# Attention into a gated unit: exponentials of one local piece by ScalarE group by group, and the first block's list of work made anew

## The chip, the cores and the metric

The kernel runs on one core of a Trainium2 chip, as one program with one launch. Its time is the device time in microseconds (us) of an execution; the median of several executions is what counts. Engines are named as in the profile: PE is TensorE with its matmuls (PEld its weight loads), DVE is VectorE, ACT is ScalarE, POOL is GpSimd, SP is SyncE, which issues the loads.

## The reference

Eight batches of eight heads of attention over 576 positions with 64 columns a head, four heads with a band of 32 positions and four that see every 32nd position; the result of all heads side by side, 4608 rows of 512, goes through a gated unit with 1536 hidden columns. All of it is float32.

```python
scores = scale * np.matmul(q, k.transpose(0, 1, 3, 2))
mask_local = (rel >= 0) & (rel < stride)
mask_strided = (rel >= 0) & (pos[None, :] % stride == pos[:, None] % stride)
scores = np.where(masks[None, :, :, :], scores, -1000000000.0)
scores = scores - np.max(scores, axis=-1, keepdims=True)
attn = np.exp(scores)
attn = attn / (np.sum(attn, axis=-1, keepdims=True) + 1e-09)
x = np.matmul(attn, v)            # then to (B * S, H * D)
gate = 1.0 / (1.0 + np.exp(-(x @ w_gate)))
return (gate * (x @ w_val)) @ w_out
```

## The kernel before, in words

**Attention by pieces.** A batch has four pieces, b.0 to b.3, each two heads: 0 and 2 are local, 1 and 3 strided. The positions that see each other are laid out so that a local piece has ten groups of 64 columns (five per head) on 128 partitions, a strided piece twelve groups of 54. Each group has a maximum and a sum of its own per partition. A piece goes through steps: Q and V load queries with keys, and values; K writes the mask into a PSUM bank by a matmul (first batch; for later ones DVE adds it, step M); S multiplies the scores onto it; A takes the maxima (DVE, one instruction for all ten groups); U subtracts them (DVE, into the SBUF tile sb); E takes the exponentials (ACT, one pass over sb, or two if the piece is in parts); N sums the groups and takes reciprocals (DVE); W multiplies (DVE, Wp on POOL); T transposes on PE and P copies out of PSUM (ACT); X weighs the values (PE); H and L split the result into a high and a low part, tiles xh and xl; R keeps the 64 positions beyond 512. In the first batch a local piece has one more column per group that holds 1e-9 (TINY), so that the sum of 65 columns has it in it; step Z sets it by a memset on POOL.

**The products.** A product with float32 weights is three matmuls in a faster type, high by high, low by high and high by low: a triple, 512 columns wide, for each of four chunks of 128 input columns. A weight block is loaded by SP (raw, 512 KB), and split by ACT, DVE and POOL in six steps (wa, wb, ws, wd, wu, wl) into a high and a low tile. Step fg f.i.c is the triple of chunk c for hidden block f, gate (i = 0) or value (i = 1); chunk order is 0, 2, 1, 3, so a product begins when piece 0 is weighed, and needs piece 1 next, then piece 2. Gate and value of a block are followed by the sigmoid and product (s, m), split (x, y) and the product with the third weight (o). Batches 3 to 7 use sums of weights to do with 7 half products what takes 8.

**What sets the order.** All steps stand in one hand-written list of names, ORDER, and each engine runs its instructions in the order in which the steps issue them; nothing else reorders them. SP's queue is the loads in list order. Step J n on PE is a matmul of n columns of ones whose result is not read: it fills time in which PE would have nothing to do. BANKS says which PSUM bank a step of the first batches uses. The first list lines hold the first two batches' attention and the first products and weights; from batch 3 on the list is regular.

The lines that the change and the steps below touch: load_qk L292, load_v L305, room L324, rows L333, soft_max L404, soft_sub L413, expo L431, norm_row L437, norm_sum L444, norm_mult L453, score L360 (matmul L371), turn L463, spread L482, weigh L493, split_high L547, split_low L551, keep_rest L559, products L587 (matmul L592), busy L722 (matmul L730), the splitting of weights L252 to L276, and the table of steps from L947 with the loop that runs the list behind it.

Of the kernel before, what the change touches and what calls it, by code (L numbers as in the profile page):

```python
# [10 lines left out]
F32 = mybir.dt.float32  # L11
# [11 lines left out]
P = 128  # L23
# [41 lines left out]
    "S0.0": "o0", "T0.0": "o1", "X0.0": "o1", "S0.1": "o1", "T0.1": "o0", "X0.1": "o0", "S0.2": "o1", "X0.2": "o1", "T0.3": "o0", "X0.3": "o0",  # L65
    "S1.0": "o1", "X1.0": "o1", "g1": "a",
# [16 lines left out]
wb0.1 wa0.1 fg1.0.0 fH0.2 ws0.1 wr3.0 wb1.1 fT0.3 fL0.2 wa1.1 wd0.1 fR0.2 wr3.2 ws1.1 fg0.0.1 fP0.3 wd1.1 fS1.0 wu0.1 wu1.1 wl0.1 wb0.2 wlp1.1 fg1.0.1
fM1.0 fQ1.1 wa0.2 fg0.1.0 fA1.0 wr4.0 fg0.0.2 wa2.1 fU1.0 fg0.1.1 wb2.1 ws2.1 fX0.3 fE1.0 wr4.2 ws0.2 wdp2.1 wb1.2 fn1.0 fg1.1.0 fH0.3 fN1.0 wu2.1
fg0.1.2 fL0.3 fWp1.0 wa1.2 fg1.1.1 fR0.3 ws1.2 wr5.0 fg1.0.2 wlp2.1 fB1.0.1 fg0.0.3 fg0.1.3 fB1.0.0 s0.0 wdp0.2 fg1.0.3 wb2.2 m0.0 wa2.2 fg1.1.2
wdp1.2 fB1.0.2 x0.0 wr5.1 fg2.0.0 s0.1 fg2.1.0 y0.0 wu0.2 fg2.0.1 wu1.2 fB1.0.3 wa3.0 fg1.1.3 wb3.0 ws2.2 fZ1.1 fg2.1.1 m0.1 wdp2.2 wr5.2 fg2.0.2
# [96 lines left out]
TINY = 1e-9  # L183
# [4 lines left out]
def attention_then_glu(ctx, tc, qk_l, qk_s, v_l, v_s, w_all, consts, out):  # L188
# [89 lines left out]
    def pair(b, step, space):  # L278
# [789 lines left out]
```

## Time and profile before

| | us |
|---|---|
| runs shown (3) | 926.85, 927.66, 929.27 |
| median | 927.66 |
| profiled execution | 929.75 |
| its span | 927.6 |
| PE busy | 919.8 (99% of the span) |
| DVE busy | 599.9 (65%) |
| ACT busy | 426.8 (46%) |
| POOL busy | 179.9 (19%) |
| mean granted clock of PE | 0.996 |

The span runs from the first to the last instruction of the profiled execution; the 2.15 us between it and the execution's time lie around it. In rows of the timeline the first number is the start in us from the span's beginning, the second the time to the group's end, then engine, line, operation, what it writes and reads, and in brackets the idle time before it with what ended it. Rows of groups show in place of the start and time the busy time and the mean ns of one instruction. PE's granted clock is given as a share of full speed.

### The profile page before, as it was taken

To read this page: it belongs to the slowest core of one execution; us is meant where nothing else is said; L and a number is where in the kernel's file an instruction comes from. 1 tells how busy PE (TensorE), PEld (TensorE's weight loads), DVE (VectorE), ACT (ScalarE), POOL (GpSimd) and SP (SyncE) were. 2 spreads that over 40 slices of the span, in tenths; PEclk is the share of its full clock that TensorE was granted. 3 is DMA by queue.
4 is the path that set the end of the run, shared out by engine and by line. 5 is a ranking of instruction groups with operands and counts; after the bars stand their busy time and mean duration, and the time that the engine had idled before them with its cause. 6 is when DMAs were issued, how large, how long until landed. Compare 5 with 4: busy or idle time off the path is not lost.

```text
span 927.6 us, 18516 instructions
## 1 busy us (share of the span) xinstructions
PE 919.8 (99%) x7606; PEld 754.9 (81%) x7606; DVE 599.9 (65%) x959; ACT 426.8 (46%) x776; POOL 179.9 (19%) x243
## 2 busy tenths in 40 slices
PE   8999999999999999999999999999999999999998
PEld 5788888888888888888888888888888888888886
DVE  5898877667799899665667896766248333333331
ACT  5888754334546455443435544444335233332222
POOL 4452641554555321000000210000003000000000
PEclk9899999999999999999999999999999999999999
DMA  9862644465677455655645436654443055444111
GB/s 345 333 220 85 197 152 153 159 192 159 199 240 247 115 187 191 208 189 181 193 157 181 149 109 195 198 181 148 138 156 125 23 174 178 145 150 146 59 45 46
DMA packets 90195, 154.19 MB, mean 166 GB/s; under 512 B 5888, under 2 KB 40192, under 8 KB 90112
## 3 DMA queue, kind: packets, MB, share of 16 engines
q1 hardware_dynamic: 89712, 152.36, 50.9%
q8 instruction: 60, 0.98, 0.4%
q10 hardware_dynamic: 400, 0.66, 0.3%
q14 instruction: 23, 0.19, 0.1%
HBM read 121.53 MB, written 31.46 MB: 165 GB/s over the span
## 4 chain that ended last, share of the span: by engine, by line
PE 98%; ACT 1%; DVE 1%; issue 0%; POOL 0%; DVEq 0%; ACTq 0%; POOLq 0%
PE o L623 22%; PE p L887 21%; PE d L887 16%; PE g L592 10%; PE v L592 10%; PE o_a L623 5%; PE o_g L623 3%; PE o_v L623 3%; PE x_a L513 2%; PE x L513 1%; PE s_g L371 1%; PE s_v L371 1%; PE gv L592 1%; PE s L371 1%; PE unread L730 0%; ACT sb L435 0%
## 5 line engine op out<-in xcount | busy, mean ns | idle before, releaser
L887 PE MATMUL p<-xs,ring 128*128 128x512 f32 x864 | 204.6, 389 | 0.0
L887 PEld LDWEIGHTS p<-xs,ring 128*128 128x128 f32 x864 | 162.2, 188 | 33.7
L623 PE MATMUL o<-w,hh 128*128 128x512 f32 x576 | 180.6, 395 | 0.0
L887 PE MATMUL d<-xs,ring 128*128 128x512 f32 x648 | 155.6, 389 | 0.0
L887 PEld LDWEIGHTS d<-xs,ring 128*128 128x128 f32 x648 | 121.6, 188 | 25.2
L623 PEld LDWEIGHTS o<-w,hh 128*128 128x128 f32 x576 | 106.1, 188 | 22.7
L480 DVE STREAM_TRANSPOSE pt<-sb 32x320 f32<-32x320 f32 (+1 forms) x224 | 120.1, 536 | 4.5
L623 PE MATMUL o<-w,hl 128*128 128x512 f32 x288 | 112.0, 389 | 0.0
L921 DVE TENSOR_TENSOR e<-e,d 128x512 f32<-128x512 f32 x54 | 37.1, 687 | 110.6 <-PE d L887 62.5
L592 PE MATMUL g<-xh,w 128*128 128x512 f32 x256 | 85.9, 393 | 0.0
L916 ACT COPY e<-p 128x512 f32<-128x512 f32 x54 | 31.7, 587 | 116.8 <-PE p L887 116.8
L592 PE MATMUL v<-xh,w 128*128 128x512 f32 x256 | 85.2, 390 | 0.0
L623 PEld LDWEIGHTS o<-w,hl 128*128 128x128 f32 x288 | 54.1, 188 | 11.5
L592 PEld LDWEIGHTS g<-xh,w 128*128 128x128 f32 x256 | 48.5, 189 | 10.3
L592 PEld LDWEIGHTS v<-xh,w 128*128 128x128 f32 x256 | 48.0, 188 | 10.0
L815 POOL TENSOR_TENSOR sum<-sum 128x128 f32<-128x128 f32 x96 | 51.5, 540 | 6.3
L592 PE MATMUL g<-xl,w 128*128 128x512 f32 x128 | 50.3, 393 | 0.3 <-DVE xl L553 0.3
L616 DVE TENSOR_TENSOR hl<-hid,hh 128x512 fp32r<-128x512 f32 x36 | 28.0, 780 | 34.5 <-ACT hh L612 34.3
L592 PE MATMUL v<-xl,w 128*128 128x512 f32 x128 | 49.8, 389 | 0.0
L810 POOL TENSOR_TENSOR sum<-w 128x256 f32<-128x256 f32 x44 | 35.5, 827 | 72.7 <-DMA sets<-sum 49.4
L929 ACT ACTIVATE e<-e 128x512 f32<-128x512 f32 x54 | 34.2, 633 | 29.9 <-DVE e L921 29.9
L612 ACT CAST hh<-hid 128x512 fp32r<-128x512 f32 x36 | 22.4, 622 | 49.9 <-PE o_a L623 41.1
(164 smaller groups left out, 1416.6 us busy)
## 6 DMA issues: line engine op xcount, KB each, us to landing
ring<-sets SPq DMA_DIRECT2D x126, 512.0 KB, 4.1
raw<-in_w_all SPq DMA_DIRECT2D x36, 512.0 KB, 5.8
vv<-in_v_l SPq DMA_DIRECT2D x15, 640.0 KB, 4.6
qk<-in_qk_l SPq DMA_DIRECT2D x14, 608.0 KB, 5.2
qk<-in_qk_s SPq DMA_DIRECT2D x14, 594.0 KB, 6.0
out<-ob SPq DMA_DIRECT2D x32, 256.0 KB, 2.0
sets<-w SPq DMA_DIRECT2D x24, 256.0 KB, 3.3
sets<-sumh SPq DMA_DIRECT2D x24, 256.0 KB, 2.8
```

Of the source, the lines that this page charges most:

```text
L371: nc.tensor.matmul(sc[j % len(sc)][g * m : (g + 1) * m, j // len(sc) * BANK + (s - lo) * kk : j // len(sc) * BANK + (s - lo + 1) * kk], q[ ...
L480: nc.vector.transpose(dst[to : to + LB, :, col : col + LB], src[part * LB : (part + 1) * LB, :, h * LB : (h + 1) * LB])
L513: nc.tensor.matmul(at_bank(r, (u * per + g) * m, (u * per + g + 1) * m)[j * D : (j + 1) * D], v[part][rows, slot * P + j * D : slot * P + ...
L592: nc.tensor.matmul(o, w, x, start=first and n == 0, stop=last and n == len(todo) - 1)
L616: by.tensor_tensor(hl, whole_h.pop((k, f)), hh.bitcast(F32), op=ALU.subtract)
L623: nc.tensor.matmul(acc[k][i], h[:, i * P : (i + 1) * P], w, start=f == 0 and n == 0, stop=f == NF - 1 and n == 2,)
L810: nc.gpsimd.tensor_tensor(u[:, at : at + 2], part(wh[f][i], c), part(wl[f][i], c), op=ALU.add)
L815: nc.gpsimd.tensor_tensor(u[:, to], u[:, x], u[:, y], op=op)
L887: nc.tensor.matmul(to, w[:, (wi * 2 + c) * P : (wi * 2 + c + 1) * P], x[xi][:, c], start=p in (1, 2, 5) and c == j == 0, stop=c == 1 and j ...
L916: nc.scalar.copy(x, two[m, 0])
L921: nc.vector.tensor_tensor(x, x, two[m, 1], op=ALU.add)
L929: nc.scalar.activation(x, x, AF.Sigmoid)
```

## The change

In piece 2 of batch 0 (local) DVE no longer subtracts the maxima and no longer sums. A step G (max_neg, POOL) writes minus scale times the maxima into columns of mxs, which is twice as wide; then the step E finds them and does, in place of one pass over sb, ten activations of 64 columns each. Each reads its scores from PSUM, has its column of negated maxima as the bias, writes its group of sb, and adds the group's exponentials up into a column (accum_out). POOL adds TINY to the ten sums. Step N of that piece is then only DVE's reciprocal. The other pieces take the old path. Step Z with its memset is as it was.

```diff
 BANKS = {
-    "S0.0": "o0", "T0.0": "o1", "X0.0": "o1", "S0.1": "o1", "T0.1": "o0", "X0.1": "o0", "S0.2": "o1", "X0.2": "o1", "T0.3": "o0", "X0.3": "o0",
-    "S1.0": "o1", "X1.0": "o1", "g1": "a",
+    "Sa0.0": "o0", "X0.0": "o0", "S0.1": "o1", "T0.1": "o0", "S0.2": "o0", "S0.3": "o0", "T0.3": "o1", "S1.0": "o1", "S1.1": "o1", "g1": "o0",
 }
...
-fAa0.0 wr1.1 fSa0.1 fA0.0 fQ1.0 wr0.2 fUa0.0 wr2.1 fS0.1 fU0.0 fEa0.0 wr1.2 fK0.3 fE0.0 fA0.1 wb2.0 wa2.0 fU0.1 wr4.1 fN0.0 fE0.1 J1024 fK0.2 fS0.2 fN0.1
...
+fP0.1 wa2.0 wd0.1 J384 fK0.2 wu0.0 ws2.0 fS0.2 wu0.1 wlp0.0 wb2.0 fX0.1 fA0.2 wr4.1 fN0.3 fH0.1 fG0.2 wlp0.1 fE0.2 J224 fS1.0 fL0.1 fWp0.3 fg0.1.0 fQ1.1 fM1.0
+fg0.0.0 fA1.0 wdp2.0 fR0.1 fN0.2 wb1.0 fW0.2 wa1.0 wu2.0 ws1.0 wr3.1 fT0.2 wb2.1 wd1.0 wlp2.0 fg0.1.1 fP0.2 fU1.0 wu1.0 fT0.3 fg1.1.0 fP0.3 fX0.2
...
-    mxs = pool.tile([P, 64], F32, name="mxs")
+    mxs = pool.tile([P, 128], F32, name="mxs")
...
+        def max_neg():
+            row = rows()[1]
+            neg = mxs[:, 64 + 16 * step : 64 + 16 * step + 2 * ns]
+            nc.gpsimd.tensor_scalar_mul(neg, row, -SCALE)
+            todo["neg"] = neg
+
+        def expo_groups():
+            prob, row, _ = rows()
+            scores = scores_of(None).rearrange("p j (t k) -> p j t k", k=kk)
+            neg = todo.pop("neg")
+            for j in range(2):
+                for t in range(ns):
+                    n = j * ns + t
+                    nc.scalar.activation(
+                        prob[:, n], scores[:, j, t], AF.Exp, bias=neg[:, n : n + 1], scale=SCALE, accum_out=row[:, n : n + 1]
+                    )
+            nc.gpsimd.tensor_scalar_add(row, row, TINY)
+            todo["row"] = row
+            todo["tiny"] = True
+
...
         def expo(part=None):
+            if "neg" in todo:
+                return expo_groups()
             prob = rows()[0]
...
             row = todo.pop("row")
-            if wide == kk:
+            if wide == kk and "tiny" not in todo:
                 nc.vector.tensor_scalar_add(row, row, TINY)
             nc.vector.reciprocal(row, row)
...
-        fE=in_parts("E"), fn=first_steps("NR"), fN=first_steps("NS"), ...
+        fG=first_steps("G"), fE=in_parts("E"), fn=first_steps("NR"), fN=first_steps("NS"), ...
```

The list is made anew from its first name up to where batch 2's products begin, and in parts behind that; later only a few of the steps e and d (copying a result out and storing it) trade places. The columns of J sum to 3552 before and 3136 now. What the list does to the engines is seen in the rows below, an engine's instructions in program order. A name ends in the piece and a buffer's number (t0_2 is the transposed block of batch 0, piece 2; qk1_0 the queries and keys of batch 1, piece 0; x the weighed values; v0_0, g0_0 and gv0_1 products).

On PE, from the first transposes of piece 2 on, before:

```order
L513 MATMUL x0_0_380<-pt0_0_271,vv0_0_127 64x32 x36
L467 MATMUL t0_2_429<-ident_62,pt0_2_342 128x128 x4
L471 MATMUL t0_2_429<-ident_62,pt0_2_342 64x64 x2
L592 MATMUL g0_0_446<-xh0_75,w0_0_377 128x512
L592 MATMUL g0_0_446<-xl0_76,w0_0_377 128x512
L592 MATMUL g0_0_446<-xh0_75,w0_0_377 128x512
L513 MATMUL x0_2_452<-pt0_2_342,v0_2_132 64x32 x32
L513 MATMUL x0_2_452<-pt0_2_342,u0_2_134 64x32 x4
L592 MATMUL gv0_1_494<-xh0_75,w1_0_340 128x512
L592 MATMUL gv0_1_494<-xl0_76,w1_0_340 128x512
```

And now, from the weighing of piece 1 on:

```order
L534 MATMUL x0_1_393<-pt0_1_340,vv0_1_180 64x54 x22
L751 MATMUL unread_82<-ones_80 128x224
L370 MATMUL s1_0_444<-qk1_0_203 32x64 x40
L613 MATMUL v0_0_489<-xh0_75,w0_1_389 128x512
L613 MATMUL v0_0_489<-xl0_76,w0_1_389 128x512
L613 MATMUL v0_0_489<-xh0_75,w0_1_389 128x512
L613 MATMUL g0_0_498<-xh0_75,w0_0_350 128x512
L613 MATMUL g0_0_498<-xl0_76,w0_0_350 128x512
L613 MATMUL g0_0_498<-xh0_75,w0_0_350 128x512
L488 MATMUL t0_2_519<-ident_62,pt0_2_511 128x128 x4
```

The transposes of piece 2 stood ahead of the first triple; now the scores of the next batch's piece 0 (40 matmuls from qk1_0) and two triples, for value and gate, stand ahead of them. Before, those scores came behind the first three triples.

On DVE, the stretch that holds piece 2's multiplication (pt0_2), before, from the maxima of piece 2:

```order
L409 TENSOR_REDUCE mxs_63<-s0_2_230 128x10
L418 TENSOR_TENSOR sb0_2_96<-s0_2_230,mxs_63 128x10x64
L265 TENSOR_SCALAR high1_0_273<-high1_0_273 128x512
L265 TENSOR_SCALAR words2_0_219<-words2_0_219 128x512
L441 TENSOR_REDUCE mxs_63<-sb0_2_96 128x10
L451 RECIPROCAL mxs_63<-mxs_63 128x10
L265 TENSOR_SCALAR high0_0_320<-high0_0_320 128x512
L409 TENSOR_REDUCE mxs_63<-s0_3_214 128x12
L459 TENSOR_TENSOR pt0_2_342<-sb0_2_96,mxs_63 128x640
```

And now, from the same maxima:

```order
L408 TENSOR_REDUCE mxs_63<-s0_2_347 128x10
L462 TENSOR_REDUCE mxs_63<-sb0_3_93 128x12
L472 RECIPROCAL mxs_63<-mxs_63 128x12
L574 TENSOR_TENSOR xl0_76<-x0_1_393,xh0_75 128x16x18
L574 TENSOR_TENSOR xl0_76<-x0_1_393,xh0_75 128x16x12
L574 TENSOR_TENSOR xl0_76<-x0_1_393,xh0_75 128x16x2
L389 TENSOR_TENSOR sb1_0_495<-s1_0_444,cst_61 128x640
L410 TENSOR_REDUCE mx1_0_496<-sb1_0_495 128x10
L472 RECIPROCAL mxs_63<-mxs_63 128x10
L480 TENSOR_TENSOR pt0_2_511<-sb0_2_96,mxs_63 128x640
```

Subtraction and sum of piece 2 are gone; its reciprocal and multiplication now stand behind the low part of piece 1, and behind the mask and the maxima of the next batch's piece 0 (sb1_0, mx1_0).

On ACT, the ten groups in their place now:

```order
L570 CAST xh0_75<-x0_1_393 128x16x18
L570 CAST xh0_75<-x0_1_393 128x16x12
L570 CAST xh0_75<-x0_1_393 128x16x2
L439 ACTIVATE sb0_2_96,mxs_63<-s0_2_347,mxs_63 128x64 x10
L583 COPY xr0_77<-x0_1_393 128x2x18
L583 COPY xr0_77<-x0_1_393 128x2x12
```

The ten groups, shown as one row, are behind the casts of piece 1 and ahead of its left-over columns; their rows wait for POOL's multiplication by minus scale.

On SP, the loads from the first values on, before:

```order
L316 DMA vv0_1_122<-in_v_s 128x768
L316 DMA vv0_0_127<-in_v_l 128x1280
L312 DMA v0_2_132<-in_v_l 128x1024
L312 DMA u0_2_134<-in_v_l 128x256
L312 DMA v0_3_161<-in_v_s 128x768
L236 DMA raw0_1_163<-in_w_all 128x1024
L236 DMA raw1_1_178<-in_w_all 128x1024
L303 DMA qk1_0_193<-in_qk_l 128x1216
```

And now:

```order
L315 DMA vv0_1_180<-in_v_s 128x768
L311 DMA v0_2_183<-in_v_l 128x1024
L311 DMA u0_2_185<-in_v_l 128x256
L302 DMA qk1_0_203<-in_qk_l 128x1216
L311 DMA v0_3_206<-in_v_s 128x768
L235 DMA raw1_0_209<-in_w_all 128x1024
```

The queries of batch 1 (qk1_0) stood behind five weight blocks and the values of all four pieces; they now stand behind four weight blocks (raw1_1, raw0_1, raw0_0 and raw2_0) and the values of pieces 0 to 2. The values of piece 3 and block raw1_0 come right after them.

More of the change, by code (lines that the diff above doesn't have):

```diff
@@ L83 @@
[L83 to L86, printed above, removed]
@@ L131 @@
[L131 removed]
+J0 K fZ0.0 fZ0.1 fQa0.0 fZ0.3 fZ0.2 fQb0.0 fQa0.1 fQb0.1 fQ0.3 C J384 fK0.1 fK0.0 wr1.1 fKa0.0 fV0.0 fQ0.2 fSa0.0 wr0.1 wr0.0 fS0.0 fAa0.0 wr2.0 fSa0.1 fV0.1
+fUa0.0 fV0.2 fA0.0 fEa0.0 fS0.1 fU0.0 fK0.3 fQ1.0 fA0.1 fV0.3 fE0.0 wr1.0 fN0.0 wr2.1 J352 fS0.3 wr0.2 wr1.2 fWp0.0 fA0.3 wa1.1 fU0.3 wb1.1 J576 fT0.0 fU0.1
+fE0.3 wr3.2 ws1.1 fP0.0 fE0.1 wd1.1 J320 fX0.0 wu1.1 fN0.1 wlp1.1 fH0.0 fV1.0 fR0.0 wb0.1 fL0.0 wa0.1 fW0.1 wa0.0 wr3.0 ws0.1 J896 fT0.1 wb0.0 ws0.0 wd0.0 wr2.2
@@ new lines @@
+y0.9 o0.8 wu11.0 ws10.2 wlp11.0 fL1.2 fB1.3.3 s0.10 wdp10.2 wa11.1 fg10.1 wb11.1 ws11.1 wu10.2 wd11.1 wlp10.2 fB1.3.2 o0.9 m0.10 wu11.1 x0.10 wl11.1
+y0.10 wa11.2 fB1.3.0 wb11.2 fg11.0 fB1.3.1 ws11.2 wd11.2 fg11.1 s0.11 wu11.2 wlp11.2 fX1.3 pa0.0.1 m0.11 o0.10 fH1.3 LV0 x0.11 fL1.3 pb0.0.1 fR1.3
+y0.11 g1.0 pa0.0.0 pb0.0.0 pl0 v1.0 s1.0 oh0.11.0 m1.0 x1.0 S0.0 e0.0 y1.0 d0.0 oh0.11.1 LQ1 M0.0 M0.1 D0 A0 g1.1 e0.2 U0 d0.2 e0.1 E0 d0.1 N0 v1.1
+s1.1 W0 e0.3 g1.2 ph0.0.0.1 d0.3 m1.1 B0.1 x1.1 y1.1 ph0.0.1.0 B0.0 v1.2 s1.2 B0.2 B0.3 o1.0 Z1 m1.2 pw0.0.0 x1.2 pw0.0.1 pd0.0.0 y1.2 pd0.0.1 X0.0
@@ new lines @@
+oh2.2.0 m2.3 Z7 pw4.1.1 x2.3 X6.0 pw5.0.0 pd4.1.1 y2.3 pd5.0.0 S7.0 LV7 H6 R6 xh3.1.1 oh2.2.1 LQ8 M7.0 M7.1 pa5.0.1 A7 g2.4 D7 U7 pa5.1.0 xl3.1.1 E7
+pb5.0.1 N7 v2.4 s2.4 W7 pb5.1.0 ph5.0.1.1 B7.0 g2.5 m2.4 B7.1 x2.4 ph5.1.0.0 B7.2 v2.5 B7.3 y2.4 pw5.0.1 s2.5 oh2.3.0 pw5.1.0 pd5.0.1 m2.5 pd5.1.0
+X7.0 x2.5 y2.5 S8.0 LV8 H7 R7 pa5.1.1 oh2.3.1 xh3.1.2 LQ9 M8.0 M8.1 A8 o2.4 pb5.1.1 D8 U8 xl3.1.2 E8 ph5.1.1.1 N8 g2.6 W8 B8.0 v2.6 s2.6 B8.1 B8.2
+B8.3 oh2.5.0 m2.6 Z9 pw5.1.1 X8.0 x2.6 pd5.1.1 y2.6 S9.0 LV9 H8 R8 xd3.0.0 oh2.5.1 LQ10 M9.0 M9.1 D9 A9 g2.7 xh3.0.5 U9 xl3.0.5 E9 N9 v2.7 s2.7 W9
@@ new lines @@
+xd3.1.2 xl3.1.3 D12 xh3.1.6 A12 xh3.1.7 xl3.1.6 xl3.1.7 o2.11 xd3.1.3 U12 e2.0 xh3.1.4 d2.0 e2.1 E12 xl3.1.4 d2.1 G3.0.1 N12 e2.2 V3.0.1 W12 d2.2
+c3.0.0.1 B12.0 G3.0.2 r5 c3.0.1.1 B12.1 V3.0.2 ad3.0.0.2 B12.2 sg3.0.2 G3.0.6 r6 ad3.0.1.2 mu3.0.2 V3.0.6 c3.0.0.6 B12.3 x3.0 G3.0.5 r7 c3.0.1.6 y3.0
+Z13 e2.3 V3.0.5 d2.3 G3.0.7 r8 V3.0.7 c3.0.0.7 ad3.0.0.7 G3.0.4 c3.0.1.7 sg3.0.7 ad3.0.1.7 V3.0.4 sg3.0.4 mu3.0.7 G3.0.3 r9 mu3.0.4 x3.1 V3.0.3
+ad3.0.0.3 y3.1 sg3.0.3 oh3.0.0 r10 ad3.0.1.3 mu3.0.3 X12.0 S13.0 LV13 H12 R12 oh3.0.1 LQ14 M13.0 M13.1 D13 A13 G3.1.1 U13 V3.1.1 c3.1.0.1 E13 G3.1.2
@@ new lines @@
+N13 r11 c3.1.1.1 W13 V3.1.2 ad3.1.0.2 B13.0 G3.1.6 sg3.1.2 r12 ad3.1.1.2 V3.1.6 c3.1.0.6 B13.1 G3.1.5 B13.2 r13 c3.1.1.6 V3.1.5 B13.3 mu3.1.2 G3.1.7
+x3.2 y3.2 V3.1.7 c3.1.0.7 ad3.1.0.7 G3.1.4 r14 c3.1.1.7 sg3.1.7 ad3.1.1.7 V3.1.4 sg3.1.4 mu3.1.7 G3.1.3 r15 mu3.1.4 x3.3 V3.1.3 ad3.1.0.3 y3.3 sg3.1.3
+o3.1 r16 ad3.1.1.3 mu3.1.3 X13.0 S14.0 LV14 H13 R13 o3.2 LQ15 M14.0 M14.1 A14 D14 U14 G3.2.1 E14 N14 V3.2.1 c3.2.0.1 W14 G3.2.2 r17 c3.2.1.1 B14.0
+V3.2.2 ad3.2.0.2 B14.1 sg3.2.2 G3.2.6 r18 ad3.2.1.2 B14.2 V3.2.6 c3.2.0.6 B14.3 G3.2.5 c3.2.1.6 mu3.2.2 Z15 x3.4 V3.2.5 y3.4 G3.2.7 r19 V3.2.7
```

98 lines of the change are left out of this document (41 added, 57 removed).

## The prediction

> **What bounds the kernel now.** I read the page first, then the table of stretches of two microseconds, then the timeline of PE in the first 50 us, and last the queues that feed it.
>
> ```profile
> PE 919.8 (99%) x7606; PEld 754.9 (81%) x7606; DVE 599.9 (65%) x959; ACT 426.8 (46%) x776; POOL 179.9 (19%) x243
> ...
> 22.00:24.00 2.00, 1.68 (x14) 1.11 (x9) 1.66 (x5) 1.85 (x6) 1.50 (x2) 0.94 1.01 405
> 24.00:26.00 2.00, 2.00 (x42) 1.35 (x41) 1.72 (x4) 1.14 (x2) 0.73 (x1) 0.50 1.05 413
> ...
> 30.00:32.00 2.00, 2.00 (x85) 1.44 (x83) 0.75 (x2) 1.93 (x5) 0.00 (x0) 0.86 1.04 415
> ```
>
> PE is busy for 99% of the span. The stretches (after the stretch: busy time of PE, PEld, DVE, ACT, POOL, then the granted clock, DMA share and GB/s) show part of the rest: the granted clock, 0.94 in 22:24, is 0.50 from there to 30:32, which has 0.86; the low stretch is from about 23.8 to 30.6 us.
>
> ```profile
> 15.73 0.87 PE L467 MATMUL t<-ident,sb 128*128 128x128 f32 x6 [0.58 <-POOL sb L459]
> 16.44 0.60 PE L730 MATMUL unread<-ones 128*128 128x256 f32 x2
> ...
> 22.00 0.66 PE L467 MATMUL t<-ident,pt 128*128 128x128 f32 x4
> ...
> 22.82 0.49 PE L592 MATMUL g<-xh,w 128*128 128x512 f32 x1
> ...
> 23.63 0.71 PE L592 MATMUL g<-xl,w 128*128 128x512 f32 x1 [0.32 <-DVE xl L553]
> ...
> 24.70 2.13 PE L513 MATMUL x<-pt,v 64*64 64x32 f32 x58
> ...
> 27.11 0.79 PE L592 MATMUL gv<-xh,w 128*128 128x512 f32 x1
> 28.56 1.48 PE L467 MATMUL t<-ident,sb 128*128 128x128 f32 x6
> 29.69 0.78 PE L592 MATMUL g<-xh,w 128*128 128x512 f32 x1
> 30.97 1.04 PE L371 MATMUL s<-qk 64*32 64x64 f32 x80
> 31.93 0.50 PE L592 MATMUL gv<-xh,w 128*128 128x512 f32 x1
> ...
> 34.88 0.91 PE L513 MATMUL x<-pt,v 54*64 54x54 f32 x44
> 35.72 0.50 PE L592 MATMUL gv<-xh,w 128*128 128x512 f32 x1
> ...
> 45.46 1.35 PE L513 MATMUL x<-pt,vv 64*64 64x32 f32 x72
> 46.74 0.50 PE L592 MATMUL v<-xh,w 128*128 128x512 f32 x1
> ...
> 52.88 2.72 PE g L592 x12
> ```
>
> The last wait of PE for another engine is the 0.32 us at 23.63. From there PE runs without a gap, and a triple of product matmuls takes 2.72 / 4 = 0.68 us. So the kernel's time is PE's own work plus what PE loses before that point: only the start can matter. I take one mark, the end of the weighing of piece 3 of batch 0, 35.72 us. Up to it both lists give PE the same real work: scores, transposes and weighing of the four pieces, the scores of the next batch's piece 0, and seven triples. A new list is worth the difference at this mark, if PE does not wait later.
>
> The low clock has a price here: the weighing of piece 2 took 24.70 to 27.11 = 2.41 us against 1.28 at 45.46 to 46.74, a triple 27.11 to 28.56 = 1.45 against 0.68, the six transposes 1.13 against 0.71 (15.73 to 16.44), the next triple 1.28 against 0.68. Together 1.13 + 0.77 + 0.42 + 0.60 = 2.9 us.
>
> **The exponentials by groups.** Gone from DVE are one subtraction and one sum, 0.83 us each, and from ACT one pass of 0.74; the memset of the column for TINY stays.
>
> ```profile
> 15.04 0.83 DVE L418 TENSOR_TENSOR sb<-s,mxs 128x640 f32<-128x640 f32 x1
> 16.67 0.83 DVE L441 TENSOR_REDUCE mxs<-sb 128x10 f32<-128x650 f32 x1
> ...
> L435 ACT ACTIVATE sb<-sb 128x640 f32<-128x640 f32 x2 | 1.5, 739 | 2.1 <-DVE sb L418 1.6 <-DVE sb L420 0.5
> L435 ACT ACTIVATE sb<-sb 128x384 f32<-128x384 f32 x1 | 0.5, 525 | 0.0
> 20.66 0.33 ACT L562 COPY xr<-x 128x36 f32<-128x36 f32 x3
> ...
> L329 POOL MEMSET sb<- 128x10 f32 x2 | 0.2, 116 | 0.3 <-POOLq L1056 0.3
> 17.54 0.22 DVE L451 RECIPROCAL mxs<-mxs 128x10 f32<-128x10 f32 x1
> ```
>
> ACT gets ten instructions of 64 columns instead. From 739 ns at 640 and 525 ns at 384 columns a column costs 0.84 ns and an instruction 0.20 us, so a group is 0.26 us by itself. Lower end: three short copies of about 0.19 us took 0.33 us together, so neighbours overlap by some 0.11 us, 0.15 us a group, 1.5 us in all. Upper end: no row has a per-row bias or a sum as output; if the sum must be read out in a step of its own of 0.20 us, 0.46 a group, 4.6 us. I take 0.36, 3.6 us, nearer the upper end because both unknowns only add. POOL gets two operations on ten columns, each between 0.12 (its memset of that size) and 0.34 (DVE's reciprocal of ten, 0.22, times 1.27 / 0.83, what a whole multiplication takes on POOL and on DVE, rows below); I take 0.3.
>
> [...]
>
> **The loads.** The scores of the next batch now stand before the first product on PE, so the load of their queries decides.
>
> ```profile
> 15.91 0.33 SPq L303 DMA_DIRECT2D qk<-in_qk_l  x1
> ...
> DMA to landing us min/median/max: 9.8/9.8/9.8
> ```
>
> It was issued at 15.91 and landed 9.8 us later, at 25.7. The queue is full throughout (405 to 415 GB/s in the stretches above), so a landing goes by the bytes ahead. The new list puts one weight block (512 KB) and one block of values (384 KB) behind it: 0.92 MB at 0.41 MB/us is 2.2 us, so it lands at 23.5, give or take 0.5. PE arrives where the old list stood after the same scores, transposes and weighings, 22.0 to 22.1, and waits 1.4 us; the scores take 0.96 (30.97 to 31.93) and end at 24.46, two triples follow, 25.82.
>
> **DVE and the sums.** Next on PE are the transposes of piece 2, which need its normalized block. On DVE that multiplication is behind the mask and the maximum of the next batch's scores.
>
> ```profile
> 32.10 0.82 DVE L390 TENSOR_TENSOR sb<-s,cst 128x640 f32<-128x640 f32 x1
> ...
> 32.96 0.82 DVE L411 TENSOR_REDUCE mx<-sb 128x10 f32<-128x640 f32 x1
> ...
> 18.69 1.44 DVE L459 TENSOR_TENSOR pt<-sb,mxs 128x640 f32<-128x640 f32 x1
> ...
> 24.62 0.83 DVE L459 TENSOR_TENSOR sb<-sb,mxs 128x648 f32<-128x648 f32 x1
> ...
> 14.40 1.27 POOL L459 TENSOR_TENSOR sb<-sb,mx 128x648 f32<-128x648 f32 x1 [0.60 <-ACT low L261]
> 16.34 1.33 POOL L269 TENSOR_TENSOR high<-high,low 128x512 int32<-128x512 int32 x1 [0.67 <-DVE high L265]
> 17.12 0.65 ACT L261 ACTIVATE low<-raw 128x512 int32<-128x512 uint32 x1
> 17.68 0.82 ACT L489 COPY pt<-t 128x512 f32<-128x512 f32 x2
> 18.41 0.61 ACT L273 CAST w<-high 128x512 fp32r<-128x512 f32 x1
> 18.93 0.58 ACT L489 COPY pt<-t 128x512 f32<-128x512 f32 x1
> ...
> 20.08 0.69 ACT L549 CAST xh<-x 128x288 fp32r<-128x288 f32 x3
> ```
>
> The mask starts 0.17 us after the scores (31.93 to 32.10), at 24.63, and mask and maximum take 0.86 each (32.10 to 32.96): DVE is free at 26.35. The subtraction and sum that were saved are no gain at this place, since DVE would wait for the load anyway. The other input comes from ACT: the groups stand behind the three casts of piece 1 (0.69), which follow its weighing at about 21.9, so they run from 22.6 to 26.2, and POOL's addition makes it 26.6. The later one counts. Reciprocal 0.22, then the multiplication: 0.83 with POOL idle (24.62), 1.44 beside POOL's work (18.69); POOL starts piece 3's multiplication (1.27) at this moment, so I take 1.2. PE gets the block at 28.05, after 2.2 us idle. This is where the stall goes: no gap at 23.63, but one of 1.4 us at 22.1 and one of 2.2 us at 25.8.
>
> **To the mark.** Transposes 0.82 (22.00 to 22.82), triple 0.68, six transposes 0.71, triple 0.68, weighing 1.28, three triples 2.04: 34.26. The weighing of piece 3 needs the bank that piece 2's result is read from. Ahead of the last reading of it ACT's queue has, behind the groups, four splits of weights (0.56 each from start to start, 17.12 to 17.68), two casts (0.52), two pairs of copies (0.73), one pass of 640 (0.74), and 0.33, 0.59 and 0.22 for the left-over columns and the bank's own cast and copy: 6.6 us, plus about 1.4 in which a cast waits for POOL (1.27 + 1.33 after 26.6): 34.2, and DVE's low half 0.69 later, 34.9. The weighing ends 0.84 us after that (34.88 to 35.72), at 35.75. Against 35.72 the sum is nothing: the new list gains the 2.9 us of low clock and gives them back in waits. Later I cost the remade list at nothing: PE had no wait after 23.63 in the old list, so its buffers of weights and pieces were ahead of it there, and the new list does the same work; a late weight would cost its whole lateness.
>
> The profiled execution took 929.75 us with a span of 927.6, so the sum gives 929.75 in its own terms. The timed runs go from 926.85 to 929.27, median 927.66; the lowest is 2.9 below the profiled one, just the price of the low clock, so I read them as executions with more or less of it. If the new list has none of it, its runs lie between 927.7 (all of the 2.1 us comes from profiling) and 929.8 (none does). I take the middle, **928.8 us**, 0.12% above the median.
>
> **Rivals.** Slower: the group costs 0.5 us or more, because each sum is read out before the next group starts. From 0.36 on every 0.1 us moves the groups' end, and all that follows, by 1 us: at 0.55, 1.9 us, 930.7. For it: ten short instructions with two operands of unknown price; against: 3.6 us is already near the upper bound. Slower too: the low clock comes back in the 2.2 us gap. [...] For it: the drop at 23.8 stands behind a gap of only 0.32 us; against: full-width triples stand on both sides of the gap.
>
> [...]
>
> Faster: groups of 0.15 us and loads 0.5 us early leave DVE as the only bound; the block comes at 27.2, 0.9 earlier, and the bank wait goes with it: 927.2 to 927.9. More than that needs the two gaps gone, 3.6 us, so 925.2 or less. The change not doing what it says is also open: the sums come from ACT only if that path is taken, else DVE does 0.83 more at 26.6 and the result is 929.6.
>
> **Chances.** The forecast has 0.44, the costly group 0.20, the low clock in the gap 0.10, the mild gain 0.12, the gain beyond both gaps 0.14. A measurement of this kernel tells about 0.3% from no change, 2.8 us: faster means below 924.9, slower above 930.4. Faster is the last case, 0.14. Slower is two thirds of the costly group and half of the low clock, and 0.06 for a late weight out of the forecast: 0.24. The rest, 0.62, is no change. The range is 924.9 to 931.6: below, the gaps gone; above, the upper end of the group (4.6 us, so 1 us) together with a profiled-level start and the low clock.
>
> **What would show it.** In the profile of the changed kernel: ten ACT rows of 64 columns with starts about 0.36 us apart; a wait of PE on the query load near 22 us and one on DVE near 26 us; DVE's multiplication of piece 2 near 26.8; no 0.50 clock between 22 and 28 us; PE without a gap after 35 us. I am wrong if the weighing of piece 3 ends more than 1 us from 35.75, if PE waits again after it, or if the groups are under 0.2 us.

## The result

The changed kernel took 937.88 us (median of 4, 935.13 to 939.50) against 927.93 for the one before (4 runs): a ratio of 1.0105, 95% interval 1.0090 to 1.0121. It is 10 us slower; 928.8 was predicted, with a range up to 931.6. The profiled execution took 938.94 with a span of 937.2, 9.6 us more than the span before.

The time is lost in two places. In PE's timeline the weighing of three pieces (strided piece 3 of batch 0, whose end was the prediction's mark, and then two later pieces) gives the lag. Of the kernel before (the row of the first, 34.88, stands in the prediction; the two rows in the middle are used further down):

```profile
236.46 0.91 PE L513 MATMUL x_a<-pt,vv 54*64 54x54 f32 x44
...
267.00 0.73 PE L623 MATMUL o<-w,hh 128*128 128x512 f32 x2
...
269.17 0.61 PE L623 MATMUL o<-w,hh 128*128 128x512 f32 x2
...
278.10 1.29 PE L513 MATMUL x_a<-pt,vv 64*64 64x32 f32 x69
```

And of the changed kernel:

```profile
37.32 0.91 PE L534 MATMUL x<-pt,v 54*64 54x54 f32 x44
...
238.95 0.91 PE L534 MATMUL x_a<-pt,vv 54*64 54x54 f32 x44
...
287.38 1.29 PE L534 MATMUL x_a<-pt,vv 64*64 64x32 f32 x69
```

The lag is 37.32 - 34.88 = 2.44 us, still 2.49 at 239 us, and 9.28 at 287. So 2.4 us are lost in the first 40 us, and 6.8 between 239 and 287 us, where the prediction had nothing. The end adds 0.3. The 2.4 us are counted from a run of the kernel before that had lost 2.9 us to the low clock itself; beside a run without that, the start loses some 5 us.

**The start.** PE's timeline of the changed kernel around the mark:

```profile
18.81 0.85 PE L488 MATMUL t<-ident,sb 128*128 128x128 f32 x6 [0.69 <-DVE sb L480]
...
20.60 0.43 PE L357 MATMUL s<-cst 128*128 128x320 bf16 x2 [0.30 <-ACT pt L510]
...
22.70 0.65 PE L751 MATMUL unread<-ones 128*128 128x224 f32 x2
23.28 1.04 PE L370 MATMUL s<-qk 64*32 64x64 f32 x80
...
29.12 1.09 PE L488 MATMUL t<-ident,pt 128*128 128x128 f32 x4 [3.21 <-DVE pt L480]
...
31.93 1.07 PE L488 MATMUL t<-ident,sb 128*128 128x128 f32 x6
```

PE did not wait for the queries: unread matmuls ran until 23.28, and the scores of the next batch followed at once. The wait is at 29.12: 3.21 us for piece 2's block, where 2.2 were forecast. What feeds it, on ACT, POOL and DVE:

```profile
23.43 0.34 ACT L439 ACTIVATE sb<-s,mxs 128x64 f32<-128x64 f32 x1
23.64 0.22 ACT L439 ACTIVATION_READ_ACCUMULATOR sb<-s,mxs 128x1 f32 x1
23.73 0.34 ACT L439 ACTIVATE sb<-s,mxs 128x64 f32<-128x64 f32 x1
...
26.24 0.28 ACT L439 ACTIVATION_READ_ACCUMULATOR sb<-s,mxs 128x1 f32 x1
...
26.69 0.25 POOL L442 TENSOR_SCALAR mxs<-mxs 128x10 f32<-128x10 f32 x1 [2.23 <-ACT sb L439]
27.02 1.27 POOL L480 TENSOR_TENSOR sb<-sb,mxs 128x648 f32<-128x648 f32 x1
28.25 1.85 POOL L268 TENSOR_TENSOR words<-words 128x512 int32<-128x512 int32 x1
...
25.27 0.82 DVE L410 TENSOR_REDUCE mx<-sb 128x10 f32<-128x640 f32 x1
26.97 0.22 DVE L472 RECIPROCAL mxs<-mxs 128x10 f32<-128x10 f32 x1 [0.88 <-POOL mxs L442]
27.23 1.75 DVE L480 TENSOR_TENSOR pt<-sb,mxs 128x640 f32<-128x640 f32 x1
```

A group is two instructions, the activation and one that reads out its sum (the accumulator), and groups start 0.29 us apart, 2.9 us for ten. POOL's two small steps take 0.26 and 0.25. DVE's multiplication, 0.83 us alone, takes 1.75 beside POOL's work. Behind the wait the granted clock is at half from 29.0 to 32.4, as the stretches of one us show (columns as in the prediction's stretches):

```profile
28.00:29.00 1.00, 0.00 (x0) 0.00 (x0) 1.00 (x2) 0.00 (x0) 1.00 (x2) 1.00 1.03 417
29.00:30.00 1.00, 0.88 (x4) 0.72 (x4) 1.00 (x1) 0.00 (x0) 1.00 (x1) 0.51 0.99 397
...
32.00:33.00 1.00, 1.00 (x8) 1.00 (x7) 1.00 (x2) 0.49 (x1) 0.26 (x1) 0.78 1.02 407
33.00:34.00 1.00, 1.00 (x19) 0.59 (x20) 0.54 (x1) 0.96 (x3) 0.00 (x0) 1.00 1.03 409
```

**The later loss.** PE's waits between 100 and 400 us, of which the kernel before had none (what waits, for what: us in all, times, longest):

```profile
PE o L644 <- DVE ob L660: 1.5, 1, 1.5
PE g L613 <- ACT e L621: 1.0, 1, 1.0
PE x_a L534 <- DVE pt L501: 0.7, 1, 0.7
PE s_v L370 <- DVE e L626: 0.5, 1, 0.5
```

They add up to 3.7 us, all between 253 and 275. Behind the last one the clock is at half again, from 274.8 to 278.2, and PE goes slower:

```profile
274.68 1.15 PE L644 MATMUL o<-w,hh 128*128 128x512 f32 x2 [1.52 <-DVE ob L660]
...
278.43 0.62 PE L644 MATMUL o<-w,hh 128*128 128x512 f32 x2
```

Nine matmuls take 3.75 us (274.68 to 278.43); in the kernel before the same nine took 2.17 (267.00 to 269.17). That is 1.6 us. Set place by place beside the old timeline, the waits move PE's work by more than their rows say: by 1.19 us where the row has 0.66, by 1.15 where it has 0.99, and by 2.53 around the rows of 0.53 and 1.52. That is 4.9 us in all, and with the 1.6 of low clock and 0.3 in small steps it makes the 6.8.

### The profile page after: what moved, and what is told of

It is laid out like the page before. It is cut to its first block, busy times and chain, and to the rows that moved or that the text cites. A ratio compares the mean times of both kernels' runs of the same rounds, so it can differ in the third digit from the quotient of the medians.

```text
span 937.2 us, 18520 instructions
## 1 busy us (share of the span) xinstructions
PE 921.6 (98%) x7604; PEld 755.3 (81%) x7604; DVE 600.2 (64%) x965; ACT 430.1 (46%) x795; POOL 166.6 (18%) x237
## 4 chain that ended last, share of the span: by engine, by line
PE 90%; DMA 4%; POOL 2%; ACT 2%; DVE 1%; issue 1%; SPq 1%; POOLq 0%; ACTq 0%; DVEq 0%
PE p L908 21%; PE o L644 20%; PE d L908 16%; PE g L613 8%; PE v L613 8%; PE o_a L644 5%; PE o_g L644 3%; PE o_v L644 3%; PE x_a L534 2%; DMA sets<-sum 1%; PE x L534 1%; PE s L370 1%; POOL sum L836 1%; DMA out<-ob 1%; PE s_g L370 1%; PE s_v L370 1%
## 5 line engine op out<-in xcount | busy, mean ns | idle before, releaser
L637 DVE TENSOR_TENSOR hl<-hid,hh 128x512 fp32r<-128x512 f32 x36 | 28.0, 780 | 34.5 <-ACT hh L633 34.3
```

Source lines behind the costliest of these rows:

```text
L637: by.tensor_tensor(hl, whole_h.pop((k, f)), hh.bitcast(F32), op=ALU.subtract)
```

## The experiments

Each run has its median, and its ratio to the kernel before, timed beside it on the same chip. The letters in the expectations name the theories that a run should tell apart. The clock of a run is the mean of PE's granted clock over the whole run; it does not say where the low stretch lies.

| run | median us | ratio (95%) |
|---|---|---|
| changed kernel | 937.88 | 1.0105 (1.0090 to 1.0121) |
| r1 new start, old rest | 932.74 | 1.0051 (1.0036 to 1.0067) |
| r2 old start, new rest | 932.66 | 1.0054 (1.0036 to 1.0072) |
| r4 r1 with less POOL | 931.77 | 1.0036 (1.0023 to 1.0049) |
| r6 r4 with the gap filled | 931.31 | 1.0045 (1.0029 to 1.0062) |
| r8 r1 with the old exponentials | 933.42 | 1.0066 (1.0051 to 1.0081) |
| r7 old list, groups | 934.03 | 1.0077 (1.0062 to 1.0092) |
| r5 changed, cast moved | 935.55 | 1.0092 (1.0077 to 1.0107) |
| r9 changed, eight moves | 938.30 | 1.0117 (1.0099 to 1.0136) |
| r12 r2, cast moved | 931.15 | 1.0039 (1.0026 to 1.0052) |
| r11 r2, eight moves | 933.08 | 1.0060 (1.0043 to 1.0077) |
| r15 r2, other buffer | 936.01 | 1.0096 (1.0074 to 1.0119) |
| r13 r12, other buffer | 933.72 | 1.0056 (1.0041 to 1.0072) |
| r16 before, copies out moved | 935.81 | 1.0076 (1.0056 to 1.0095) |
| r10 before, gap filled | 927.02 | 0.9998 (0.9989 to 1.0008) |

**r1 and r2: the list cut in two.** Both lists hold the same steps up to one place (names 516 and 517; some steps are on another engine, and the groups and the steps J differ), so the halves can be exchanged.

```diff
-ORDER = after[:517] + after[517:]
+r1: after[:517] + before[516:]
+r2: before[:516] + after[517:]     # with the old step U0.2
```

> The changed kernel with its remade first block (about the first 50 us and the weights' preparation up to the first product of hidden block 0 for batch 1), and the list of before from there on. Theory A (two separate losses: 2.4 us at the start, and 6.8 us between 238 and 288 us that come from how the list orders the copies out and the sums of weights there): 2.4 us over before, 929.5 to 931.5, no PE wait after 40 us. Theory B (the later loss follows from the start, which hands the later part on in another state): the waits near 250 to 275 us stay, 936 to 938.

> The kernel before, old exponentials and old first block, with the changed list from the first product of batch 1 on. Theory A: only the later loss, 6 to 7 us over before, 933.5 to 935.5, with PE's waits near 250 to 275 us. Theory B: like before, 927 to 929.

Two losses that do not depend on each other: 0.51% and 0.54%, together the 1.05% of the change. r1 keeps the 3.2 us wait for piece 2 and has 0.4 us of waits later; r2 has none of the 3.2 us, and waits of 3.3 us in all behind 100 us, at 248 to 271. Theory A holds; its sizes were off. r1's eight runs go with their mean granted clock: 929.5 and 929.9 at 1.000, 932.6 to 934.5 at 0.995 to 0.998, where the kernel before took 926.7 to 927.5 at 1.000. So the start loses about 2.6 us at the full clock, and 3 to 5 us more in the runs with a lower clock. The clock explains the larger part of these: r1's profiled run, at 0.996, has it at half from 28.4 to 35.2 us, behind the same wait and twice as long as the changed kernel's, which is 3.4 us of work at most. The low clock of the profiled run of the kernel before was the exception: 14 of its 17 runs beside r1 have 0.998 or more.

**r4: POOL's work beside the multiplication.**

```diff
-... fG0.2 wlp0.1 fE0.2 J224 fS1.0 fL0.1 fWp0.3 fg0.1.0 ... fA1.0 wdp2.0 fR0.1 fN0.2 wb1.0 fW0.2 ...
+... fG0.2 wlp0.1 fWp0.3 fE0.2 J224 fS1.0 fL0.1 fg0.1.0 ... fA1.0 fR0.1 fN0.2 wb1.0 fW0.2 wd2.0 ...
```

> As r1, but on POOL piece 3's multiplication stands ahead of the addition of TINY, and the joining of weight block 2's words is done by DVE behind piece 2's multiplication, so that POOL has no block-wide work beside DVE's multiplication of piece 2 (1.75 us in the changed kernel, 0.83 with POOL idle). Theory C (POOL's work beside it is what makes DVE's multiplication slow): it takes 0.8 to 0.9 us, PE's wait for it is 2.2 to 2.4 us in place of 3.2, and the start ends some 0.9 us earlier. Theory D (it is slow by itself, through what it reads or writes): 1.7 us again, no change against r1.

DVE's timeline of r4:

```profile
26.82 0.82 DVE L480 TENSOR_TENSOR pt<-sb,mxs 128x640 f32<-128x640 f32 x1
```

0.82 in place of 1.75, PE's wait 2.29 in place of 3.21, and 1.0 us less in the median than r1, though the intervals overlap. Theory C holds by its trace. r4 takes both of POOL's steps away from beside the multiplication, so it does not say which of them counts; POOL and DVE of r8 (below), where only one is beside it, show that one is nearly enough:

```profile
27.31 1.27 POOL L275 TENSOR_TENSOR w<-words,w 128x512 fp32r<-128x512 f32 x1 [0.73 <-ACT w L272]
...
27.71 1.56 DVE L480 TENSOR_TENSOR pt<-sb,mxs 128x640 f32<-128x640 f32 x1
```

**r6: the gap filled.**

```diff
-fL0.1 fg0.1.0
+fL0.1 J1152 fg0.1.0
```

> As r4, with 1152 columns of unread matmuls (about 2 us) on PE ahead of the first product, so that PE's 2.3 us of waiting for piece 2 are filled. No work is late by it, if it ends before the block comes. Theory F (the wait itself costs the granted clock): no 0.50 clock behind it, 1.7 to 3.4 us less than r4, 928.5 to 930. Theory G (the clock falls there for another reason): the low clock stays, 931 to 933.

Stretches of r6:

```profile
26.00:28.00 2.00, 2.00 (x13) 1.47 (x12) 1.97 (x4) 1.18 (x3) 0.19 (x1) 1.00 1.02 409
28.00:30.00 2.00, 2.00 (x18) 1.45 (x18) 2.00 (x3) 2.00 (x6) 1.28 (x1) 1.00 1.04 418
```

All four runs have 0.999 or 1.000, and the 2.3 us wait is gone; r4 has 0.997 or 0.998 in five of its ten runs. That fits F, but with half of r4's runs free of the low clock too, four runs do not prove it. The time did not fall (the ratios of r4 and r6 overlap, and 931.31 lies in G's range, not in F's): r4 at 1.000 took 928.95 to 929.96, r6 930.1 to 931.7, so the filler cost about a microsecond, which F did not foresee. What it made late I did not trace.

**r8 and r7: the groups by themselves.** r8 is r1 with fU0.2 in the place of fG0.2, r7 the kernel before with fG0.2 in the place of fU0.2 (and the new functions).

> As r1 (new start, old rest), with the old exponentials of piece 2: DVE subtracts, ACT does one pass, DVE sums. Theory J (in this order the sum is late on ACT, so groups cost): DVE gets 0.83 + 0.83 us more, ACT 2.2 less; subtraction ends near 24.5, pass near 25.3, mask and maxima of the next piece end near 27, sum and reciprocal 28.1, multiplication from there beside POOL: PE's wait is about 1 us longer than r1's 3.2, 933 to 935. Theory K (POOL's part and the ten groups are the late ones): the wait is shorter, 930 to 932.

> The list of before, with only the exponentials of piece 2 done by groups: POOL's multiplication by minus scale in the place of DVE's subtraction, ten groups on ACT in the place of one pass. Ten groups take 2.9 us on ACT where one pass takes 0.74, so ACT is 2.2 us later at the copies of piece 1's transposes, on which PE waits. Theory H (groups cost what ACT is late): 1.5 to 2.5 us over before, 929 to 930. Theory I (DVE's 1.7 us less make up for it, since DVE's low part was PE's last wait): within 0.7 us of before, 927 to 928.

In the new list the groups cost nothing: without them PE's wait is 3.6 us in place of 3.2, the sign of J at less than half its size, and the two intervals overlap. The runs at a low clock are alike too: r1's three at 0.995 or 0.996 took 932.75 to 934.48, r8's four 933.18 to 933.46. In the old list the groups cost 0.77%, 6.9 us in the median, some three times what H said. PE's timeline of r7:

```profile
19.59 0.66 PE L489 MATMUL t<-ident,pt 128*128 128x128 f32 x4 [2.46 <-ACT sb L440]
```

And its stretches of two us:

```profile
18.00:20.00 2.00, 0.41 (x4) 0.42 (x4) 0.02 (x1) 2.00 (x13) 0.26 (x1) 1.00 1.04 401
20.00:22.00 2.00, 1.81 (x27) 0.98 (x29) 2.00 (x3) 2.00 (x6) 1.55 (x2) 0.70 1.04 419
...
30.00:32.00 2.00, 2.00 (x26) 1.54 (x21) 0.71 (x2) 1.33 (x3) 0.00 (x0) 0.50 1.05 422
...
34.00:36.00 2.00, 2.00 (x84) 1.28 (x84) 1.03 (x2) 2.00 (x6) 0.54 (x1) 0.89 0.65 262
```

PE waits 2.46 us for bank o1: the groups read their scores straight from PSUM and hold the bank until the last of them, and in the old table the transposes of piece 0 use the same bank. DVE's subtraction, which ends at 15.87 before (15.04 + 0.83), had set it free 3.6 us sooner. Behind that wait the clock is at half from 20.8 to 34.5 us (the shares 0.70 and 0.89 give the ends), though PE is busy but for 0.19 us; the larger part of the loss is put down to that, without a run that separates it from the wait.

**r5, r12, r9, r11: the casts of sums.** What the trace of the changed kernel shows ahead of its first late wait, on ACT and DVE:

```profile
241.66 0.62 ACT L841 CAST sumh<-sum 128x512 fp32r<-128x512 f32 x1 [1.07 <-POOL sum L836]
242.18 0.71 ACT L570 CAST xh<-x_a 128x288 fp32r<-128x288 f32 x3
...
242.31 0.69 DVE L845 TENSOR_TENSOR sum<-sum,sumh 128x512 fp32r<-128x512 f32 x1 [1.00 <-ACT sumh L841]
242.92 0.48 DVE L389 TENSOR_TENSOR sb<-s_g,cst 128x320 f32<-128x320 f32 x1
```

The cast of sums of weights (sumh) waits 1.07 us for POOL, the split of the piece before stands behind it on ACT, and on DVE the mask of the next piece behind the sums' low part, though its scores are there from 241.0. In the old list this cast came later, well behind the piece's maxima.

```diff
-S4.0 ph3.1.0.0 pa3.1.1 LV4 H3 pw3.1.0 R3 oh1.9.1 LQ5 M4.0 pd3.1.0 ... A4 U4 E4 g2.0
+S4.0 pa3.1.1 LV4 H3 R3 oh1.9.1 LQ5 M4.0 ... A4 ph3.1.0.0 U4 pw3.1.0 E4 g2.0 pd3.1.0
```

> The changed kernel with one block's cast and low part of the sums of weights (steps ph3.1.0.0 and pw3.1.0, and their store) moved from ahead of piece 4's mask back to behind its maxima and subtraction, as the list of before had it. Theory A2 (ACT and DVE stand at that cast, which waits for POOL's sums, with the split of the piece before and the mask of the next one queued behind it; the whole chain of the piece is then some 2 us late, and PE meets it at 252): PE's first late wait (0.66 us at 253) goes, and with it half or more of the 6.8 us, 932 to 935. Theory A3 (DVE has too much between 238 and 275 us in whatever order, or the copies out are what is late): no more than 1 us gained, 936 or more, and PE's waits at 262 and 274 stay as long.

> As r2, with only the cast of sums, its low part and store moved behind piece 4's subtraction (the edit of r5). By L: the first late waits of PE (two for the transposed blocks, 1.5 us together) go, and the later ones stay: 930 to 931.5, between r2 and r11. By M: 932 or more, like r2.

Both are a little faster, 1.0092 against 1.0105 and 1.0039 against 1.0054, with intervals that overlap; in their traces the waits for transposed blocks are gone, 0.7 us of the changed kernel's and 1.5 of r2's. The wait goes as A2 said, but not half of the loss with it, and the waits at 263 to 275 us stay, as A3 said. r12 is where L put it. PE's waits of r12 from 100 us on:

```profile
PE o L623 <- DVE ob L639: 1.5, 1, 1.5
PE g L592 <- ACT e L600: 0.7, 1, 0.7
PE s_v L371 <- DVE e L605: 0.3, 1, 0.3
```

r9 and r11 move eight names (the expectations say seven): the three of r12, and five that put the first copy out of batch 1 (e1.0) ahead of the next cast into its buffer, and that cast with its low part and store later.

> As r2 (old start, changed list behind it), with seven names of that list moved: the cast of sums of weights that stood ahead of piece 4's mask goes behind its subtraction (as in r5), and the first copy out of batch 1 with its store goes ahead of the next cast of sums into the same buffer (ost), which goes behind the left-over rows of piece 4, its low part behind the maxima of piece 5. Theory L (the later loss is made by ACT standing at these two places: at a cast that waits for POOL's sums, and at two copies out that wait for each other's store): the waits of PE at 250 to 275 us go, 927 to 929. Theory M (POOL's sums are late as a whole, in any order of these steps): 931 or more.

> The changed kernel with the seven moves of r11. By L: what is left is the loss of its start, as r1 has it, 931 to 934. By M: like r5, 935 or more.

Theory L fails here: r11 is far above its 927 to 929, 1.9 us slower than r12 in the median (the intervals overlap), and r9 is no better than the changed kernel. New waits for ACT stand in place of the old ones (1.0 us at the scores of a later piece).

**r3, r13, r15: another buffer.** r3 was to give the third copy out, e1.2, a buffer of its own, but named the one that it had already.

> The changed kernel with one edit: the third copy out of batch 1 (e1.2) goes to another staging buffer than the first (e1.0), so it needs not wait for that one's store to land. Theory A1 (ACT's 3.4 us wait in that copy is what makes the later loss): the waits of 0.99, 0.53 and 1.52 us on PE and the 1.7 us of low clock behind them go, 4 to 6 us less than the changed kernel, 932 to 934. Theory A2 (the sums of weights, which were moved between batch pieces, hold up ACT and DVE there anyway): less than 2 us gained, 936 or more.

It is the changed kernel once more, and took 938.13 beside 927.32 (1.0106): nothing on A1 or A2, but the 937.88 repeats. The edit as it was meant:

```diff
+        if (k, i) == (1, 2):
+            tag = "l0"
         if (k, i) not in given:
```

> As r12, and the third copy out of batch 1 (e1.2) goes to the staging buffer l0, where it follows the store of e1.1, in place of ost, where it follows the store of e1.0 that is issued behind it. Theory P (ACT's 3.6 us in e1.2 are what makes PE wait 1.5 us for the last copy out): that wait falls under 0.5 us and the time is 1 to 2.5 us below r12, 928.5 to 930. Theory Q (ACT's time there has slack, and DVE or the sums are late by themselves): within 0.7 us of r12's 931.15, and PE's wait stays 1 us or more.

> As r2, with only e1.2's staging buffer changed as in r13. P: 1 to 2.5 us below r2's 932.66, 930 to 931.7, the two early waits of PE for transposed blocks (1.5 us) as in r2. Q: like r2, 932 to 933.5.

P fails: neither gains. r15 is even slower than r2 by ratio, with intervals that do not touch, which Q did not foresee either. ACT's timeline of r12, at e1.2:

```profile
261.17 0.59 ACT L639 COPY ob<-o 128x512 f32<-128x512 f32 x1 [3.56 <-DMA out<-ob]
```

And of r13, at e1.2 and the next cast of sums:

```profile
258.56 0.59 ACT L641 COPY ob<-o 128x512 f32<-128x512 f32 x1 [2.16 <-DMA out<-ob]
261.35 0.62 ACT L822 CAST sumh<-sum 128x512 fp32r<-128x512 f32 x1 [2.20 <-DMA out<-ob]
```

ACT's wait in e1.2 falls from 3.56 to 2.16 us, and the next cast, which uses l0 too, waits 2.20 for e1.2's store. The wait moved one user on. (The time of r13 is spread with its clock, 929.7 at 1.000 and 934.4 at 0.996.)

**r16: the copies out alone.** The kernel before, with only e1 and d1 put where the changed list has them.

```diff
-B4.3 e1.0 pb3.1.1 d1.0 ... D5 e1.2 U5 d1.2 ... v2.1 pa4.0.0 e1.1 s2.1 W5 d1.1 ... oh2.0.0 e1.3 s2.2 pw4.0.0 d1.3
+... U5 e1.1 xl3.0.1 E5 d1.1 e1.0 N5 v2.1 d1.0 ... B5.0 e1.2 g2.2 m2.1 d1.2 ... R5 e1.3 oh2.0.1 xh3.0.2 LQ7 M6.0 d1.3
```

> The kernel before with one group of steps moved: the four copies out of batch 1 and their stores stand as in the changed list (second, first and third one close together behind piece 5's subtraction, the last one behind the left-over rows of piece 5), the sums of weights as before. Theory R (three copies out in a row on two staging buffers make ACT and DVE late by themselves): PE waits 1 us or more for the last copy out near 265, 929 to 931.5. Theory S (they are late only because the sums that the changed list put ahead of them hold buffers, ACT and POOL): no such wait, 926.8 to 928.

The copies out do make a loss by themselves, as R said, and a larger one: 0.76%. PE's wait for the last copy out is only 0.6 us, though; it waits longer elsewhere. ACT, SP and PE of r16:

```profile
256.74 0.58 ACT L639 COPY ob<-o 128x512 f32<-128x512 f32 x1 [1.00 <-DMA out<-ob]
263.59 0.62 ACT L820 CAST sumh<-sum 128x512 fp32r<-128x512 f32 x1 [6.27 <-DMA out<-ob]
...
258.55 0.49 SPq L804 DMA_DIRECT2D sets<-w  x1
259.14 0.54 SPq L786 DMA_DIRECT2D out<-ob  x1
...
266.20 0.42 PE L371 MATMUL s_g<-qk 64*32 64x64 f32 x2 [2.47 <-ACT e L600]
```

The store of e1.2 is issued at 259.14, behind eight transfers of sums on SP's queue, and the next cast of sums into the same buffer, in ACT's order ahead of a split and a sigmoid, waits 6.27 us for it to land. PE waits 2.47 us for the sigmoid, and 2.0 in three waits for transposed blocks. Behind the former the clock is at half from 265.5 to 272.3 us, so a part of the loss is clock.

**r10: the kernel before, its gap filled.** J384 ahead of fg0.0.0.

> The kernel before, with 384 columns of unread matmuls ahead of the first product, so that the 0.32 us in which PE waits between the first and the second matmul of it are filled. The granted clock of before is 1.000 to 0.998 in 14 of 17 timed runs and 0.996 in the three above 928.5. Theory N (the gaps just ahead decide whether the clock falls there): all runs at 0.999 or more, median 926.5 to 927.3. [...]

All ten runs are at 0.999 or 1.000; beside them one of 14 of the kernel before is at 0.996. That fits N, but with one low run in 14 ten without any prove little, and the median is the same. It is no faster kernel. Its profiled run, without the low clock, shows what that costs. PE's timeline of r10, at the weighing of piece 3:

```profile
31.82 1.14 PE L513 MATMUL x<-pt,v 54*64 54x54 f32 x44
```

That is 3.06 us sooner than the 34.88 of the kernel before's profiled run.

## Why the prediction was wrong

- **"Later I cost the remade list at nothing"** is the step that failed, with half of the loss (r2: 0.54%, 5.3 us). That PE had no wait after 23.63 said nothing on the new order: there was no slack in ACT and DVE for a cast or a copy out whose buffer is late. The list is remade in parts behind the first block as well; the queues of ACT and SP at those places should have been costed like those of the start. Two mechanisms are seen one at a time: a cast of sums ahead of a piece's mask (r12 takes it away: PE's 1.5 us of waits go, 1.5 us in the median, with intervals that overlap), and copies out close together in buffers whose next user waits for a store (r16 puts them into the old kernel: 7.8 us in the median, a part of it clock). They do not add up simply, and I found no small edit that takes all of r2's 5.3 us away, so how they share it stays open.
- **The base.** I took the mark of a profiled execution with 2.9 us of low clock as what the new list has to match. Few runs of the kernel before have it (3 of the 17 timed beside r1), so that 2.9 us was a credit that the median did not give. The size was right: r10 without the low clock is 3.06 us sooner at the same weighing. The forecast then took half of the 2.1 us around the span off. By the prediction's own reading nothing was to be taken off, since the lowest timed run, 926.85, is 929.75 less the 2.9. Without it the forecast is 929.75, and r1 at a clock of 1.000, with the new start alone, took 929.5 and 929.9. So the sum for the start came out, in part by luck, for the runs that keep the clock; but it was a loss of 2.6 us against most runs of the kernel before, and was told as no change. The changed kernel's own mark, with the low clock, ended at 38.16 in place of 35.75.
- **The low clock in the gap** was a rival with 0.10; it came. The clock fell at the end of the wait for one stretch of 3.4 us (29.0 to 32.4), which cost 1.4 us (the transposes took 1.37 us in place of the 0.82 of the sum, the triple 1.44 in place of 0.68, the six transposes 0.83 in place of 0.71). Six of r1's eight runs and half of r4's have a lower mean clock; with the gap filled (r6) none of four has. In r4 a wait of 2.29 us, near the 2.2 of the forecast, was followed by 3.4 us at half clock too (28.2 to 31.6), with full-width triples on both sides of it, so what stood against this rival did not hold. What the range's upper end, 931.6, counts for the low clock was the author's estimate, which no run shows: the changed kernel's stretch of 3.4 us cost 1.4, and r1's of 6.8 us 3.4 at most. Why the clock stayed at half for 13.7 us in r7, with PE busy, no run shows.
- **The group** was put at 0.36 us: 0.29, with a readout of its own, as the upper end supposed, but mostly overlapped. The costly group (0.5) falls. The groups cost nothing in this list (r8).
- **The multiplication** was put at 1.2 us: it took 1.75. r4 shows that POOL's work beside it is the cause, and by r8 one such step makes it 1.56. With the groups starting 0.8 us later than forecast and each shorter, it made the block 1.1 us late (29.12 against 28.05).
- **The loads**: the gap of 1.4 us for the queries did not appear. PE came 1.2 us later itself, after waits of 0.69 and 0.30 ahead of it; the scores ended at 24.32 (23.28 + 1.04), close to the 24.46 forecast.
- **The bank of piece 3** was no wait: the late block and the low clock had moved PE past it. The 0.65 us that the sum had for it (34.26 to 34.91) went, and hid a part of what the other terms had too low.

## What to carry to other kernels

When a list is remade in more than one place, cost each place, above all in the engines that are not the bound: an instruction that waits for a buffer holds what is behind it on its engine, as r16's cast, which waited 6.27 us for a store, held the sigmoid for which PE waited 2.47 us. Space copies out by more than the time their stores take to land, counting what stands ahead of the store on its queue: r16's store of e1.2 was issued 1.8 us after its copy had ended (257.32 to 259.14), behind eight transfers, and the cast that needed its buffer began 4.4 us after that. The fused activation with accumulated sums that reads PSUM saved DVE two passes of 0.83 us here, but held the bank until the last of its ten groups, which start 0.29 us apart, and in r7 PE waited 2.46 us for that bank; check who needs it next.

## What the runs showed of the hardware

In the changed kernel the sum of an activation over a group was read out by an instruction of its own of 0.22 to 0.28 us, which overlapped with its neighbours: the period was 0.29 us at 64 columns. DVE's multiplication of 640 columns took 0.82 us alone (r4), 1.56 beside one of POOL's block-wide steps (r8) and 1.75 beside two (changed kernel). The stretches at half clock that were measured in these runs had three lengths: 3.4 us (changed kernel at 29.0 and 274.8, r4 at 28.2), 6.8 (kernel before at 23.7, r1 at 28.4, r8 at 28.5, r16 at 265.5) and 13.7 (r7 at 20.8), that is one, two and four times 3.4. After a wait of 2.5 us the clock stayed at half for 13.7 us in r7 with PE busy nearly all the time; after one of 3.2 us in the changed kernel for 3.4 us, and in r1 for 6.8. Why the lengths differ, no run shows.
